# Moving the transposing DMA of K between the loads of K and Q and the load of V in a windowed-attention and maxout-FFN kernel

## The chip, the cores and the metric

One core of one Trainium2 chip. The metric is the device time of one execution in microseconds (us); the time before is the median of three runs. The core has the engines TensorE (PE; PEld is its weight load), VectorE (DVE), ScalarE (ACT), GpSimd (POOL) and SyncE (SP), and 16 DMA engines that take the transfers which SyncE and GpSimd issue.

## What is computed

Attention over 4 batches, 8 heads, 768 positions and a head size of 64. Each position sees the 128 positions up to its own (a sliding window) and the first 4 positions of the sequence (the sinks). The result, 3072 tokens of 512 values, goes through a feed-forward layer with three weight matrices of 512 x 768 and one of 768 x 512, the hidden value being the maximum of three products:

```python
scores = scale * np.matmul(q, k.transpose(0, 1, 3, 2))
keep = is_sink | in_window
a = softmax(np.where(keep, scores, -1e9))
x = heads_joined(np.matmul(a, v))            # 3072 x 512
h = np.maximum(np.maximum(x @ w1, x @ w2), x @ w3)
out = h @ w_out
```

## The kernel before

The 3072 tokens are cut into 12 chunks of 256, three to a batch. For each chunk the kernel loads K, Q and V (512 KB each, f32), casts them to bf16, transposes K and Q so that the head size lies on the partitions, computes scores, exponentials, masks and the weighted sum of V, transposes that sum (x_sb to xT), and runs the two layers of the feed-forward part.

The order of all instructions is written out by hand; each engine takes its own in the order of the program, and waits are put in only where data or a buffer calls for them. Up to chunk 3 the order is a long prologue. After that the loop `for i in range(3, NCH)` (L836) gives a slot to each i, and a slot works on several chunks at once: the feed-forward hidden layer of chunk i, the attention of chunk n = i + 1, the output layer of chunk m = i - 1, the cast and transpose of chunk i + 2, and the loads of chunk i + 3. Slots 4 to 10 take the branch that begins behind the `else`; the change is in that branch. A slot is named by its i below.

These parts matter for the change:

- `load(ci, what)` (L93, its DMA at L107) issues on SyncE's queue one transfer of 512 KB for each letter of `what`, by default K, then Q, then V. It does nothing for a chunk from 12 on. The raw f32 tiles have two buffers for each of K, Q and V (the pool `raw`, L51), so a load needs the cast of the chunk two before it to be over.
- `cast(ci)` (L605) is POOL's work: eight casts of K (`cast_k`, L85, at L90), then V in eight casts (`cast_v`, L121, at L129; for the chunks that the later slots cast). Where the chunk is the second of its batch, a small copy of the first keys into `ks` (`sink_k`, L278, at L283) stands between the two, and that one reads the transposed K of the chunk before. Q is cast by ACT from chunk 7 on (L953, `cast_qk`, at L118).
- `turn_dma(ci, w)` (L177) issues on SyncE's queue a transposing DMA out of the bf16 tile into `kT` or `qT` (at L188 for the chunks concerned). For K it needs POOL's eight casts. `kT` and `qT` are rings of four (L71).
- `score(n, ...)` (L314, and `score4`, L339, with its matmuls at L357) reads `kT` of chunk n and of the chunk before, and `qT`. It is the first work of TensorE in a slot, behind two small matmuls for the sinks where there are any. So `kT` of chunk i + 2, issued in slot i, is first read at the start of slot i + 1.
- `xpose_dma(n)` (L496, at L498) transposes x_sb into xT on SyncE's queue near the end of the slot; `ffn_h` (L504, matmuls at L517) reads it some us into the next slot. `store(m)` (L588) writes the output of chunk m from the same queue.

SyncE's order in a slot of 4 to 8 is therefore: qT of chunk i + 2, the loads of K, Q and V of chunk i + 3, kT of chunk i + 2, xT of chunk i + 1, the store of chunk i - 1. In the program's text the load stands at L936 and the transpose of K at L945, with `ffn_h` and `av` (other engines) between them.

Of the kernel before, what the change touches and what calls it, by code (L numbers as in the profile page):

```python
# [16 lines left out]
def kernel(  # L17
# [31 lines left out]
    with tc.manual_schedule():  # L49
# [30 lines left out]
        def keys(ci):  # L80

            return (kT[ci % RING].rearrange("q n p i r -> q (n p i r)")
                    .rearrange("q (p n h c) -> q p n h c", p=NP, n=2, h=2))
# [9 lines left out]
        def load(ci, what="kqv", gate=None, part=None, parts=1):  # L93
            if ci >= NCH:
                return
            b, c = divmod(ci, CPB)
            t0 = c * 256
            for w in what:
                src = {"k": k, "q": q, "v": v}[w]
                if (ci, w) not in raws:  # L100
                    raws[ci, w] = raw.tile([128, H, 2, D], F32, tag=w + "_raw", name=w + "_raw")
                dst = raws[ci, w]
                if gate is not None:
                    gate(dst[0:1, 0, 0, 0:1])
                n = H // parts
                for g in range(parts) if part is None else (part,):
                    nc.sync.dma_start(  # L107
                        out=dst[:, n * g:n * g + n],
                        in_=src[b, n * g:n * g + n, t0:t0 + 256]
                            .rearrange("h (p i) d -> p h (i d)", i=2))  # L110
# [66 lines left out]
        def turn_dma(ci, w):  # L177
            if ci >= NCH:
                return
            if w == "k" and ci < NEW:  # L180
                for n in range(2):
                    nc.sync.dma_start_transpose(
                        out=kT[ci % RING][:, n].rearrange("q p i r -> q (p i) r"),
                        in_=bfs[ci, w][64 * n:64 * n + 64].rearrange("q p i a d -> q (p i a d)"))
                return
            dst = (qT[ci % RING].rearrange("q p i n r -> q (p i) (n r)") if w == "q" else
                   keys(ci).rearrange("q p n h c -> q (p n) (h c)"))
            nc.sync.dma_start_transpose(  # L188
                out=dst, in_=bfs[ci, w].rearrange("s p i a d -> s (p i a d)"))
# [88 lines left out]
        def sink_k(b):  # L278
            x = (keys(b * CPB)[:, :, 0, 0].rearrange("q p (i r) -> q p i r", i=2) if b * CPB >= NEW else
                 kT[b * CPB][:, 0])  # L280
            for a in range(2):
                hp = slice(64 * a, 64 * a + 64)
                nc.gpsimd.tensor_copy(  # L283
                    ks[b % 2][hp, :, 4 * a:4 * a + 4].rearrange("q p (r i) -> q p r i", i=2),
                    x[hp, :, :, 0:2].rearrange("q p i r -> q p r i"))
# [106 lines left out]
        def expo(ci, p):  # L392
            if ci >= NEW:
                return expo4(ci, p)
            lo = 0 if ci % CPB else 1
            e, st = es[ci, p]
            for a in range(2):
                nc.scalar.activation(e[:, a, lo:], st[a][:, lo:], AF.Exp, scale=scale)  # L398
                give(st[a])
# [31 lines left out]
        def sink_v(b):  # L431

            x = vb[(b * CPB) % RING]
            sv = bank([128, 2, D + 1], F32, "sv")
            for a in range(2):
                for p in range(NP):
                    nc.tensor.matmul(
                        sv[32 * p:32 * p + 32, a], lhsT=(sel2 if b * CPB >= NEW else sel)[:, a], rhs=x[:, 0, 2 * p + a],
                        start=True, stop=True, tile_position=(0, 32 * p))
            nc.vector.tensor_copy(vs[b % 2], sv)  # L440
            give(sv)
# [129 lines left out]
        def fence():  # L571
            free.insert(0, home.pop(id(fences.pop()))[1])
# [263 lines left out]
        for i in range(3, NCH):  # L836
            n, m = i + 1, i - 1
            more = n < NCH
            if i == 3 or i >= NCH - 1:
                if more and n % CPB == 1:  # L840
                    if n < NEW:
                        sink_k(n // CPB)
                    sink_v(n // CPB)
                load(i + 3)
                cast(i + 2)
                turn_dma(i + 2, 'k')
                turn_dma(i + 2, 'q')
                if more:
                    sink_score(n)
                if more:  # L850
                    score(n, (0, 1))
                if more:
                    expo(n, 0)
                if more:
                    expo(n, 1)
                two = more and i > 3
                if two:
                    y_open(m)
                    y_turn(m, 0, 64 if n >= NEW else 128)
                else:  # L860
                    ffn_y(m, 0, nc.vector)
                if i == 3:
                    xpose(3, 0, nc.scalar)
                    xpose(3, 1, nc.scalar)
                if more:
                    score(n, (2,))
                if two:
                    fence()
                if more:
                    score(n, (3,))  # L870
                if more:
                    mask(n, 0)
                if more:
                    mask(n, 1)
                if more:
                    expo(n, 2)
                if two:
                    y_turn(m, 1, 64 if n >= NEW else 128)
                    y_out(m, 0, nc.vector)
                    y_out(m, 1, nc.vector)  # L880
                else:
                    ffn_y(m, 1, nc.vector)
                store(m)
                if more:
                    mask(n, 2)
                if more:
                    expo(n, 3)
                ffn_h(i, 0, 0)
                if more:
                    mask(n, 3)  # L890
                ffn_h(i, 0, 1)
                if more:
                    av_open(n); av(n, 0)
                ffn_h(i, 0, 2)
                if more:
                    av(n, 1)
                ffn_h(i, 1, 0)
                if more:
                    av(n, 2)
                ffn_h(i, 1, 1)  # L900
                if more:
                    av(n, 3); xpose_dma(n)
                ffn_h(i, 1, 2)
                ffn_h(i, 2, 0)
                ffn_h(i, 2, 1)
                ffn_h(i, 2, 2, 1 if i + 2 < NCH else 2)
            else:
                if more and n % CPB == 1:
                    if n < NEW:
                        sink_k(n // CPB)  # L910
                    sink_v(n // CPB)
                if more:
                    sink_score(n)
                cast(i + 2)
                turn_dma(i + 2, 'q')
                score(n, (0,))
                expo(n, 0)
                score(n, (3,))
                y_open(m)
                y_turn(m, 0, 64 if n >= NEW else 128)  # L920
                expo(n, 3)
                score(n, (1,))
                expo(n, 1)
                mask(n, 0)
                fence()
                score(n, (2,))
                y_turn(m, 1, 64 if n >= NEW else 128)
                mask(n, 3)
                expo(n, 2)
                mask(n, 1)  # L930
                y_out(m, 0, nc.vector)
                y_out(m, 1, nc.scalar)
                av_open(n)
                av(n, 0)
                mask(n, 2)
                load(i + 3)  # L936
                ffn_h(i, 1, 0)
                ffn_h(i, 0, 0)
                if more:
                    av(n, 1)  # L940
                ffn_h(i, 1, 2)
                ffn_h(i, 0, 1)
                if more:
                    av(n, 2)
                turn_dma(i + 2, 'k')  # L945
                if more:
                    av(n, 3)
                ffn_h(i, 1, 1)
                ffn_h(i, 2, 0)
                ffn_h(i, 0, 2)  # L950
                if NEW < i + 3 < NCH:
                    for g in range(2):
                        cast_qk(i + 3, "q", g, nc.scalar)  # L953
                ffn_h(i, 2, 1)
                if more:
                    xpose_dma(n)
                ffn_h(i, 2, 2, 1 if i + 2 < NCH else 2)
                store(m)
# [43 lines left out]
```

## Time and profile before

| what | value |
|---|---|
| median of three runs | 177.16 us (176.55 to 177.21) |
| the profiled execution | 177.08 us |
| its span, first to last instruction | 175.4 us |
| TensorE busy | 167.2 us, 95% |
| TensorE's granted clock | 0.999 |
| DMA moved | 34.95 MB, mean 199 GB/s |
| SyncE's DMA queue (q1) | 64784 packets, 31.33 MB |

The predictions' views are these. The page gives the busy time of each engine and the costliest groups. The view of waits names, for each engine and line, who ended its idle time, with the total in us, the number of times and the longest. The timeline lists instructions in order: start, time taken, engine, line, operation, output and inputs, and in square brackets the idle time of the engine before it and what ended that. A row with SPq is a DMA issue of SyncE; its second number is how long the issue took, not how long the transfer took. The view of DMA issues gives for each kind the count, the size and the time from the start of the issue to the landing of the data. Landing minus issue is thus time in the queue and on the way together.

### The profile page before, as it was taken

Reading aid. Unit: us, or ns where it says so; the run is one execution under the profiler, and the core shown is the slowest. Engines: PE = TensorE matmul, PEld = TensorE weight load, DVE = VectorE, ACT = ScalarE, POOL = GpSimd, SP = SyncE. Lnnn points to the kernel's source line nnn. Section 1 sums busy time; section 2 is a strip of 40 time slices with the busy share of each in tenths; the row PEclk is TensorE's granted clock in tenths of the full one; section 3 lists DMA queues with packets and bytes.
Section 4 is the critical chain, followed back from the end, with each engine's and each line's share of the span. In section 5 each row is a group of like instructions: output and inputs, shape, how many; then the busy total and the mean of one; then the engine's idle time right before and its main releaser. Section 6 shows DMA issues by size and latency. Waiting matters only on the chain.

```text
span 175.4 us, 5437 instructions
## 1 busy us (share of the span) xinstructions
PE 167.2 (95%) x2228; PEld 129.3 (74%) x2233; DVE 124.3 (71%) x262; ACT 89.6 (51%) x185; POOL 110.0 (63%) x193
## 2 busy tenths in 40 slices
PE   7979999999999999999999999997999999999992
PEld 2446879857696696797797797795797797796871
DVE  3387854896697894886877977875977777776452
ACT  4778544677945814817726627624726616510210
POOL 7399507546489999999999999586999700000000
PEclk9999999999999999999999999999999999999999
DMA  5999999999999999988999999899999605019303
GB/s 145 299 285 197 220 215 261 220 313 270 303 191 297 308 193 230 251 197 220 268 174 243 277 153 252 237 170 216 259 178 281 35 17 166 4 25 158 121 0 120
DMA packets 70505, 34.95 MB, mean 199 GB/s; under 512 B 26448, under 2 KB 68944, under 8 KB 70480
## 3 DMA queue, kind: packets, MB, share of 16 engines
q1 hardware_dynamic: 64784, 31.33, 80.4%
q0 software_dynamic: 5552, 3.15, 12.6%
q8 instruction: 17, 0.28, 0.7%
q10 hardware_dynamic: 144, 0.13, 0.2%
q14 instruction: 8, 0.07, 0.2%
HBM read 25.17 MB, written 6.29 MB: 179 GB/s over the span
## 4 chain that ended last, share of the span: by engine, by line
PE 59%; DMA 23%; POOL 9%; SPq 2%; issue 2%; ACT 2%; DVE 0%; POOLq 0%
PE h_ps L517 37%; PE y_ps L561 9%; DMA k_raw<-in_k_dram 5%; DMA kT<-k_bf 5%; DMA q_raw<-in_q_dram 4%; PE y_ps L537 4%; DMA w<-in_moe_w_dram 4%; PE o L471 3%; DMA v_raw<-in_v_dram 3%; PE st L357 3%; POOL vb L123 3%; DMA qT<-q_bf 3%; POOL vb L129 2%; POOL w L292 2%; SPq L107 1%
## 5 line engine op out<-in xcount | busy, mean ns | idle before, releaser
L517 PE MATMUL h_ps<-xT,w 128*128 128x256 bf16 x864 | 101.2, 273 | 0.5 <-DMA w<-in_moe_w_dram 0.4
L517 PEld LDWEIGHTS <-w 128*128 128x128 bf16 x864 | 81.9, 98 | 10.8 <-DMA w<-in_moe_w_dram 0.7
L527 DVE TENSOR_TENSOR h_sb<-h_sb,h_ps 128x512 bf16<-128x512 bf16 (+1 forms) x74 | 49.0, 669 | 17.8 <-PE h_ps L517 16.2
L523 ACT CAST h_sb<-h_ps 128x512 bf16<-128x512 f32 x35 | 20.6, 588 | 50.9 <-PE h_ps L517 50.8
L129 POOL CAST vb<-v_raw 32x512 bf16<-32x512 f32 x48 | 37.0, 771 | 2.3
L90 POOL CAST k_bf<-k_raw 32x512 bf16<-32x512 f32 x48 | 29.1, 607 | 4.3 <-issue 2.2
L398 ACT ACTIVATE e_sb<-st 128x512 bf16<-128x512 f32 (+1 forms) x48 | 23.2, 591 | 1.1 <-PE st L331 1.1
L479 DVE TENSOR_TENSOR x_sb<-o,rc 128x256 bf16<-128x256 f32 x48 | 20.4, 424 | 1.6
L561 PE MATMUL y_ps<-wo,h_sb 64*64 64x512 bf16 (+1 forms) x312 | 21.1, 377 | 0.0
L471 PE MATMUL o<-vb,e_sb 128*128 128x65 bf16 x352 | 16.5, 193 | 0.8 <-DVE vb L123 0.8
L471 PEld LDWEIGHTS <-e_sb 128*128 128x128 bf16 x352 | 14.5, 97 | 3.1 <-ACT e_sb L398 0.9
L123 POOL CAST vb<-v_raw 64x512 bf16<-64x512 f32 x18 | 13.1, 727 | 5.0 <-DMA v_raw<-in_v_dram 4.5
L406 DVE TENSOR_TENSOR e_sb<-e_sb,msk 128x1024 bf16<-128x1024 bf16 (+1 forms) x18 | 13.0, 747 | 3.4 <-ACT e_sb L398 3.4
L389 DVE TENSOR_TENSOR e_sb<-e_part,msk 128x1024 bf16<-128x1024 bf16 x16 | 12.9, 822 | 3.3 <-ACT e_part L374 3.1
L561 PEld LDWEIGHTS <-h_sb 64*64 64x64 bf16 (+1 forms) x312 | 9.9, 106 | 5.0
L374 ACT ACTIVATE e_part<-st 128x384 bf16<-128x384 f32 x32 | 13.1, 496 | 0.5 <-PE st L357 0.5
L537 PE MATMUL y_ps<-wo,h_sb 128*128 128x512 bf16 x49 | 12.6, 380 | 0.3
L476 DVE RECIPROCAL rc<-o 128x4 f32<-128x4 f32 x48 | 8.3, 174 | 4.0 <-PE o L471 4.0
L118 POOL CAST k_bf<-k_raw 128x512 bf16<-128x512 f32 x6 | 3.8, 648 | 9.1 <-PE h_ps L517 6.8
L118 ACT CAST q_bf<-q_raw 128x512 bf16<-128x512 f32 x13 | 7.6, 620 | 2.8 <-DMA q_raw<-in_q_dram 2.8
L537 PEld LDWEIGHTS <-h_sb 128*128 128x128 bf16 x54 | 4.9, 98 | 5.4 <-DVE h_sb L527 0.5
L427 ACT ACTIVATE e_sink<-sk 128x256 bf16<-128x256 f32 x8 | 3.1, 389 | 10.4 <-PE sk L423 10.4
(90 smaller groups left out, 144.3 us busy)
## 6 DMA issues: line engine op xcount, KB each, us to landing
k_raw<-in_k_dram SPq DMA_DIRECT2D x11, 512.0 KB, 5.6
v_raw<-in_v_dram SPq DMA_DIRECT2D x11, 512.0 KB, 7.8
out_dram<-y_sb SPq DMA_DIRECT2D x11, 512.0 KB, 3.2
q_raw<-in_q_dram SPq DMA_DIRECT2D x10, 512.0 KB, 7.5
w<-in_moe_w_dram POOLq DMA_DIRECT2D x9, 256.0 KB, 6.4
q_raw<-in_q_dram SPq DMA_DIRECT2D x4, 256.0 KB, 7.6
wo<-in_moe_w_out_dram POOLq DMA_DIRECT2D x2, 384.0 KB, 8.2
v_raw<-in_v_dram SPq DMA_DIRECT2D x2, 256.0 KB, 5.2
```

The source lines that it names most:

```text
L90: f(bfs[ci, "k"][x:x + 32, :, n], raws[ci, "k"][y:y + 32, :, i].rearrange("q (p a) d -> q p a d", a=2))
L123: eng.tensor_copy(vb[ci % RING][64 * i:64 * i + 64, n, :, 0:D], raws[ci, "v"][64 * n:64 * n + 64, :, i])
L129: eng.tensor_copy(vb[ci % RING][x:x + 32, n, :, 0:D], raws[ci, "v"][y:y + 32, :, i])
L374: nc.scalar.activation(dst, st[a], AF.Exp, scale=scale)
L398: nc.scalar.activation(e[:, a, lo:], st[a][:, lo:], AF.Exp, scale=scale)
L471: nc.tensor.matmul(o[:, t, a], lhsT=e[:, a, s], rhs=vb[cv % RING][:, n, 2 * p + a], start=first, stop=True, skip_group_check=True)
L479: nc.vector.tensor_mul(xs[ci][:, p], o[:, :, :, 0:D], rc.unsqueeze(3).to_broadcast([128, 2, 2, D]))
L517: nc.tensor.matmul(hp[:, f].rearrange("q (i t r) -> q i t r", i=2, r=x.shape[3]), lhsT=w_sb[wi][:, ds, c0:c0 + 128], rhs=x, start=(ds == 0 ...
L523: (nc.scalar.copy if eng is nc.scalar else eng.tensor_copy)(dst, hp)
L527: nc.vector.tensor_max(dst[:, x], dst[:, x], hp[:, x])
L537: nc.tensor.matmul(yp, lhsT=hs[ci][:, fb, t * 128:(t + 1) * 128], rhs=wo[:, fb], start=(fb == 0), stop=(fb == FB - 1))
L561: nc.tensor.matmul(yps[ci][t][c:c + cols], lhsT=hs[ci][hp, fb, x:x + cols], rhs=wo[hp, fb], start=(turn == 0 and fb == 0), stop=(turn == 1 ...
```

## The change

In slots 4 to 10 the call that issues the transposing DMA of K moves ahead of the load of V. The load is split in two calls for it. Nothing else is changed.

```diff
                 av_open(n)
                 av(n, 0)
                 mask(n, 2)
-                load(i + 3)
+                load(i + 3, 'kq')
+                turn_dma(i + 2, 'k')
+                load(i + 3, 'v')
                 ffn_h(i, 1, 0)
                 ffn_h(i, 0, 0)
                 if more:
@@
                 ffn_h(i, 0, 1)
                 if more:
                     av(n, 2)
-                turn_dma(i + 2, 'k')
                 if more:
                     av(n, 3)
```

SyncE's order in these slots becomes: qT of chunk i + 2, the loads of K and Q of chunk i + 3, kT of chunk i + 2, the load of V of chunk i + 3, xT of chunk i + 1, the store of chunk i - 1. For slot 9 there is no chunk 12 to load, and for slot 10 there is neither a load nor a chunk 12 to transpose.

## The prediction

> **What bounds the kernel now.** I read the page's busy times first, then TensorE's waits from 60 us on (when the twelve-chunk loop is in its steady part), then TensorE's own timeline around the one wait that is left.
>
> ```profile
> PE 167.2 (95%) x2228; PEld 129.3 (74%) x2233; DVE 124.3 (71%) x262; ACT 89.6 (51%) x185; POOL 110.0 (63%) x193
> ```
>
> ```profile
> PE st L357 <- DMA kT<-k_bf: 0.9, 1, 0.9
> PE sk L423 <- DMA qT<-q_bf: 0.2, 1, 0.2
> ```
>
> TensorE is busy 95% of the span. The second fence is the whole answer on its waits after 60 us: two waits, 0.9 us for a transposed K and 0.2 us for a transposed Q. An edit that only moves a DMA can win no more there than what TensorE waits for, so the first fact is a ceiling of about 1 us out of 177. The next fence is TensorE's timeline around the larger wait.
>
> ```profile
> 115.18 4.53 PE L517 MATMUL h_ps<-xT,w 128*128 128x256 bf16 x40
> 120.64 0.52 PE L357 MATMUL st<-qT,kT 64*64 64x256 bf16 x16 [0.93 <-DMA kT<-k_bf]
> ...
> 124.34 1.91 PE L517 MATMUL h_ps<-xT,w 128*128 128x256 bf16 x16
> ...
> 133.13 0.53 PE L357 MATMUL st<-qT,kT 64*64 64x192 bf16 x24
> ```
>
> The forty matmuls of chunk 7's slot end at 115.18 + 4.53 = 119.71. The scores of chunk 9, the first work of slot 8, start at 120.64: 0.93 us of nothing. Slot 9's scores start at 133.13. Why K of chunk 9 was late stands in SyncE's own timeline (start, time that the issue took) and in the landing column of the DMA issues of the same stretch.
>
> ```profile
> 108.24 0.64 SPq L107 DMA_DIRECT2D q_raw<-in_q_dram  x1
> 108.98 3.46 SPq L107 DMA_DIRECT2D v_raw<-in_v_dram  x1
> 112.53 3.26 SPq L188 DMA_TRANSPOSE kT<-k_bf  x1
> 116.81 1.55 SPq L498 DMA_TRANSPOSE xT<-x_sb  x1
> ...
> 119.75 1.88 SPq L188 DMA_TRANSPOSE qT<-q_bf  x1
> 121.69 0.74 SPq L107 DMA_DIRECT2D k_raw<-in_k_dram  x1
> 122.47 0.63 SPq L107 DMA_DIRECT2D q_raw<-in_q_dram  x1
> 123.21 1.16 SPq L107 DMA_DIRECT2D v_raw<-in_v_dram  x1
> 124.48 3.48 SPq L188 DMA_TRANSPOSE kT<-k_bf  x1
> ```
>
> Landings after the issue, first of slot 7 (issues of 107 to 115 us), then of slot 8 (121 to 127 us), then the one xT of 116.81:
>
> ```profile
> q_raw<-in_q_dram SPq DMA_DIRECT2D x1, 512.0 KB, 7.7
> v_raw<-in_v_dram SPq DMA_DIRECT2D x1, 512.0 KB, 9.2
> ...
> kT<-k_bf SPq DMA_TRANSPOSE x1, 8.1
> ```
>
> ```profile
> k_raw<-in_k_dram SPq DMA_DIRECT2D x1, 512.0 KB, 4.8
> q_raw<-in_q_dram SPq DMA_DIRECT2D x1, 512.0 KB, 5.8
> v_raw<-in_v_dram SPq DMA_DIRECT2D x1, 512.0 KB, 8.3
> qT<-q_bf SPq DMA_TRANSPOSE x1, 4.3
> kT<-k_bf SPq DMA_TRANSPOSE x1, 7.9
> ```
>
> ```profile
> xT<-x_sb SPq DMA_TRANSPOSE x1, 4.6
> ```
>
> Adding issue and landing: in slot 7 Q lands at 115.9, V at 118.2, kT at 120.6, xT at 121.4. In slot 8 K lands at 126.5, Q at 128.3, V at 131.5, kT at 132.4. Transfers of SyncE's queue land in the order of issue, so kT pays for all of V ahead of it.
>
> **The change part by part.** Nothing is computed differently and no instruction is added or removed. In slots 4 to 8 two issues on SyncE trade places, the load of V (chunk i+3) and the transpose of K (chunk i+2). In slot 9 no load is left (there is no chunk 12), and in slot 10 neither exists, so nothing moves there.
>
> **kT gets earlier.** Without V ahead, kT follows Q. Behind V it needed 132.4 - 131.5 = 0.9 us in slot 8 and 120.6 - 118.2 = 2.4 us in slot 7. Taking these as the two ends of its own time, the new landing in slot 7 is between 115.9 + 0.9 = 116.8 and 115.9 + 2.4 = 118.3, both ahead of the 119.71 at which TensorE is ready. I take the later end, since it is this slot's own. The 0.93 us then goes whole. The ends of the gain are 0 (if kT keeps all of the 120.6 - 115.9 = 4.7 us that it now needs after Q) and 0.93 (nothing else waits there); a loss is priced under the rivals.
>
> **What is late next at 119.71.** The rest of SyncE's work, and POOL, ACT and DVE, have to let TensorE run 0.93 us earlier from there on.
>
> ```profile
> 105.75 6.37 POOL L129 CAST vb<-v_raw 32x512 bf16<-32x512 f32 x8
> 114.33 5.17 POOL L90 CAST k_bf<-k_raw 32x512 bf16<-32x512 f32 x8 [2.21 <-issue]
> 120.71 0.44 POOL L283 COPY ks<-kT 64x16 bf16<-64x16 bf16 x2 [1.21 <-DMA kT<-k_bf]
> 121.22 6.17 POOL L129 CAST vb<-v_raw 32x512 bf16<-32x512 f32 x8
> ```
>
> ```profile
> 117.61 1.14 ACT L118 CAST q_bf<-q_raw 128x512 bf16<-128x512 f32 x2
> 121.04 2.12 ACT L374 ACTIVATE e_sb<-st 128x384 bf16<-128x384 f32 x5 [2.29 <-PE st L357]
> ```
>
> ACT sits idle 2.29 us before the exponentials, waiting for the scores, so they follow. xT (chunk 8) landed at 121.4 and is first read at 124.34; 0.93 us earlier that is 123.41, still 2.0 us behind the landing. Slot 8's kT landed at 132.4 against a need of 133.13, which becomes 132.20: in the old order 0.2 us of the gain would be given back there. In the new order it lands at 128.3 + 0.9 to 128.3 + 2.4, that is 129.2 to 130.7, and does not matter. From 133 us on the loads are over and no wait of TensorE stands in the list.
>
> **V gets later.** It is now behind kT, by kT's 0.9 to 2.4 us. In slot 7 V would land between 119.1 and 120.6. Its reader is POOL's cast, which now starts at 121.22; that start is itself 1.21 us late, because POOL stands in front of it waiting for the same kT (the copy into ks). Without that wait the cast could start at 114.33 + 5.17 + 0.44, about 120.0. So POOL waits at most 0.6 us for V where it waited 1.21 us for kT: no loss, and the cast's result is needed only two slots after the load. Cost taken: 0; if the cover goes, POOL falls behind by what V is late beyond 1.2 us.
>
> **The wait that stands in SyncE's order.** kT carries a wait for POOL's eight casts of K, and V, xT, the store and the next qT are queued behind it. In slot 7 these casts were over before 105.75, when POOL began on V; SyncE reaches the place behind Q at 108.24 + 0.64, about 108.9. In slot 8 they end at 114.33 + 5.17 = 119.50, and SyncE gets there at 123.1. So SyncE would find the K ready by 3.2 and 3.6 us, and the wait costs 0. The Trainium skill, "DMA: Bandwidth & Descriptors", section "Anatomy of one DMA — SWDGE (gpsimd) path", speaks against the move: a DMA's wait is served on the issuing sequencer before dispatch, so a transfer that waits holds back those issued after it, needed or not. By that rule V would pay for a late POOL; these rows show a POOL that is not late, so the sum stays, and the rule's other outcome is the third rival below.
>
> **xT.** The pair V and kT took SyncE from 108.98 to 115.79, and xT went out at 116.81. It can go when the DVE has written x_sb:
>
> ```profile
> 116.32 0.42 DVE L479 TENSOR_TENSOR x_sb<-o,rc 128x256 bf16<-128x256 f32 x1
> ```
>
> That is 116.74, so SyncE was not what held it, by 0.9 us. The bytes ahead of xT are the same in either order. Cost 0; without the cover each us would count only beyond the 2.0 us above.
>
> **Sum.** The profiled execution took 177.08 us (span 175.4, and 1.7 around it). Less 0.93 that is 176.15. It stood 0.08 under the median of the runs, 177.16, so the forecast on the runs' scale is **176.2**. The three runs lie 0.66 us apart (176.55 to 177.21), so a wait of this size may not be in each of them; I take 175.8 to 176.7 as the forecast's own range. About 0.5% (0.9 us) is what a measurement of this kernel can tell from no change, and the whole gain is about that.
>
> **Rival 1: kT is late for another reason than V (0.22).** A view of the DMA from 115 to 121 us shows how little was moved while kT was under way (40 slices of 0.15 us, GB/s):
>
> ```profile
> GB/s 345 311 333 251 217 179 135 72 27 20 20 20 24 15 19 72 130 9 10 10 137 394 247 239 234 118 12 0 5 9 7 12 9 10 183 90 278 295 543 301
> ...
> q14 instruction: 1, 0.01, 2.1%
> q8 instruction: 1, 0.02, 1.0%
> ```
>
> For most of 116 to 120 the engines moved 0 to 30 GB/s with two instruction fetches among their work. If a fetch on one of the 16 engines holds up a transpose that runs over all of them, kT may stay in flight until 120.6 wherever it stands in the queue. For it: 2.4 us behind V here against 0.9 in slot 8. Against it: with V out of the way kT is through Q at 115.9 and has 3.8 us until 119.71, more than the 2.4. Time: no gain, **177.1**, 176.7 to 177.5.
>
> **Rival 2: five transposes in the middle of the loads make the DMA queue the bound (0.15).** A load behind a transpose is slower to land than one behind a load: in slot 8 K landed 126.5 - 124.05 = 2.4 us after qT, Q only 1.8 us after K. That is 0.6 us more, and the new order puts V behind kT in five slots: 5 x 0.6 = 3.0 us of queue. If all of it reached TensorE (through xT, or through next loads), the time would be 177.1 - 0.9 + 3.0 = **179.2**. It decides from the point at which the queue has less than 0.6 us of idle time a slot. Against it speaks how xT lands from 60 to 140 us:
>
> ```profile
> L498 SPq DMA_TRANSPOSE xT<-x_sb x6: 1232/1232/2200, 65.8 to 130.1; - x6
> ...
> DMA to landing us min/median/max: 3.1/3.1/4.6
> ```
>
> The median is the minimum: most xT find the queue empty, and only one or two stand behind something. Two slots of 0.6 us are 1.2, inside the 2.0 us that xT has.
>
> **Rival 3: SyncE is held at kT (0.05).** If POOL ran over 3.6 us later than in the rows, SyncE would stand at kT with V, xT, the store and the next qT behind it. xT has 2.0 us more, so the first us is lost when POOL is 6.6 us late: 176.2 + 1.0 = **177.2**, and more beyond.
>
> **How the numbers follow.** Forecast 0.58, rivals 0.22, 0.15, 0.05. The forecast lies on the edge of 0.5% (176.27): of its 0.58 I give 0.42 to faster and 0.16 to the same. Rival 1 gives 0.20 to the same and 0.02 to slower, rival 2 0.15 to slower, rival 3 0.02 and 0.03. That makes faster 0.42, same 0.38, slower 0.20. The range 175.8 to 177.6 holds the forecast and rival 1 and leaves out rival 2 and the far end of rival 3.
>
> **What would show it.** Right: the profile after has no wait of PE for kT; kT in slots 4 to 8 lands 1 to 3 us after Q and ahead of V; POOL's 1.21 us wait for kT is gone or has become a shorter one for V; the span is 174.5. Wrong: a wait of PE st for kT still near 120 us with kT in flight over 4 us behind Q (rival 1); xT landing over 3.1 us after its issue in most slots and waits of h_ps for xT (rival 2); SyncE standing in front of kT for POOL (rival 3).

## The result and the profile after

| | before | after |
|---|---|---|
| median of 22 runs each | 176.62 us (175.88 to 178.22) | 176.13 us (175.80 to 177.03) |
| profiled execution | 177.08 us | 176.05 us |
| span | 175.4 us | 174.3 us |

The ratio after to before is 0.9963, with a 95% interval of 0.9946 to 0.9981: faster by 0.37%, which is 0.65 us. The two medians differ by 0.49 us, and the interval, 0.34 to 0.95 us, holds both. The forecast was 0.93 us and 176.2. The prediction called a change of less than 0.5% the same: by that border the measured 0.37% counts as the same, although its interval leaves out no change at all. In the profiled execution 1.0 us went.

The change shows first in SyncE's timeline of slot 7, after: kT stands between Q and V.

```profile
108.17 0.71 SPq L107 DMA_DIRECT2D q_raw<-in_q_dram  x1
108.98 4.96 SPq L188 DMA_TRANSPOSE kT<-k_bf  x1
113.98 0.58 SPq L107 DMA_DIRECT2D v_raw<-in_v_dram  x1
116.76 1.23 SPq L498 DMA_TRANSPOSE xT<-x_sb  x1
```

Their landings, counted from the issue, after (DMA issues of 107.5 to 114.5 us, then the one xT):

```profile
q_raw<-in_q_dram SPq DMA_DIRECT2D x1, 512.0 KB, 7.6
v_raw<-in_v_dram SPq DMA_DIRECT2D x1, 512.0 KB, 5.8
kT<-k_bf SPq DMA_TRANSPOSE x1, 7.6
```

```profile
xT<-x_sb SPq DMA_TRANSPOSE x1, 3.9
```

Q lands at 108.17 + 7.6 = 115.8, kT at 116.6, V at 119.8, xT at 120.7. Before, kT landed at 120.6. It is 4.0 us earlier in these two executions, of which only the first 0.9 us can be used. TensorE's timeline, after, across the same place:

```profile
115.12 4.53 PE L517 MATMUL h_ps<-xT,w 128*128 128x256 bf16 x40
119.58 0.52 PE L357 MATMUL st<-qT,kT 64*64 64x256 bf16 x16
```

No bracket, so no idle time: the scores of chunk 9 follow the matmuls of slot 7 directly. The view of TensorE's waits from 69 us on is empty in this profile. POOL's timeline, after, shows where V's delay went:

```profile
100.47 5.16 POOL L90 CAST k_bf<-k_raw 32x512 bf16<-32x512 f32 x8
106.91 6.90 POOL L129 CAST vb<-v_raw 32x512 bf16<-32x512 f32 x8 [1.27 <-DMA v_raw<-in_v_dram]
114.16 5.17 POOL L90 CAST k_bf<-k_raw 32x512 bf16<-32x512 f32 x8 [0.35 <-POOL vb L129]
119.40 0.45 POOL L283 COPY ks<-kT 64x16 bf16<-64x16 bf16 x2
119.90 0.61 POOL L129 CAST vb<-v_raw 32x512 bf16<-32x512 f32 x1
```

POOL's 1.21 us in front of the ks copy are gone. Instead it now stands 1.27 us ahead of 106.91, for the V that slot 6 loaded. Before, it idled 2.21 us ahead of 114.33; the profile names no releaser there, but the next K landed at 107.40 + 6.8 = 114.2. So the new wait is taken out of that one, of which 0.35 us is left, and the K casts start at 114.16, no later than they did.

### The profile page after: what moved, and what is told of

It reads as the page before. It is cut to its first block, busy times and chain, and to the rows that moved or that the text cites. A ratio compares the mean times of both kernels' runs of the same rounds, so it can differ in the third digit from the quotient of the medians.

```text
span 174.3 us, 5433 instructions
## 1 busy us (share of the span) xinstructions
PE 167.1 (96%) x2228; PEld 129.3 (74%) x2233; DVE 124.6 (71%) x262; ACT 89.6 (51%) x185; POOL 110.5 (63%) x193
## 4 chain that ended last, share of the span: by engine, by line
PE 68%; DMA 18%; POOL 7%; issue 2%; SPq 1%; ACT 1%; DVE 0%; POOLq 0%
PE h_ps L517 43%; PE y_ps L561 11%; DMA k_raw<-in_k_dram 4%; DMA q_raw<-in_q_dram 4%; PE o L471 4%; DMA w<-in_moe_w_dram 4%; PE y_ps L537 4%; PE st L357 3%; DMA v_raw<-in_v_dram 3%; DMA qT<-q_bf 3%; POOL vb L123 3%; POOL w L292 2%; SPq L107 1%; PE st L331 1%; POOL k_bf L118 1%
## 5 line engine op out<-in xcount | busy, mean ns | idle before, releaser
L517 PE MATMUL h_ps<-xT,w 128*128 128x256 bf16 x864 | 101.2, 273 | 0.6 <-DMA w<-in_moe_w_dram 0.4
L517 PEld LDWEIGHTS <-w 128*128 128x128 bf16 x864 | 81.8, 98 | 11.0 <-DMA w<-in_moe_w_dram 0.9
L129 POOL CAST vb<-v_raw 32x512 bf16<-32x512 f32 x48 | 37.5, 781 | 4.0 <-DMA v_raw<-in_v_dram 1.3
L389 DVE TENSOR_TENSOR e_sb<-e_part,msk 128x1024 bf16<-128x1024 bf16 x16 | 13.4, 862 | 3.1 <-ACT e_part L374 3.0
```

Source lines behind the costliest of these rows:

```text
L129: eng.tensor_copy(vb[ci % RING][x:x + 32, n, :, 0:D], raws[ci, "v"][y:y + 32, :, i])
L389: nc.vector.tensor_mul(x.rearrange("q a (t s) c -> q (a t) s c", t=2), y, msk2)
L517: nc.tensor.matmul(hp[:, f].rearrange("q (i t r) -> q i t r", i=2, r=x.shape[3]), lhsT=w_sb[wi][:, ds, c0:c0 + 128], rhs=x, start=(ds == 0 ...
```

## Experiments

The question was whether the one wait of TensorE is the whole difference, why only 0.65 us of 0.93 came, and whether place or bytes decide. All ratios are against the kernel before in the same set of runs. A second measure turned out to be far sharper than the clock: **the stretch** from TensorE's first sink scores of slot 4 to the end of its last matmul. Two rows of TensorE's timeline give it, here for the kernel after:

```profile
68.28 0.29 PE L423 MATMUL sk<-qT,ks 128*32 128x256 bf16 x4
...
169.52 1.47 PE L583 MATMUL y_ps<-wo,h_sb 128*128 128x256 bf16 x12
```

169.52 + 1.47 - 68.28 = 102.71 us; from unrounded times 102.72. It leaves out the prologue, whose end, read as the start of the stretch, moved between 68.1 and 71.0 us from one profiled execution to the next, more than the effect sought.

**kT ahead of V in slot 7 alone** (shown against the kernel before).

```diff
-                load(i + 3)
+                early = i == 7
+                load(i + 3, 'kq')
+                if early:
+                    turn_dma(i + 2, 'k')
+                load(i + 3, 'v')
...
-                turn_dma(i + 2, 'k')
+                if not early:
+                    turn_dma(i + 2, 'k')
```

> kT ahead of V in slot 7 alone, the old order in slots 4, 5, 6 and 8. Theory (the one wait behind slot 7 is the whole difference): as fast as the change, ratio about 0.996 to 0.998 against before, no wait of TensorE for kT of chunk 9; slot 8, in the old order, may give back up to 0.2 us. Rival (the gain comes from the sum of small shifts of transfers in all five slots): ratio within 0.999 to 1.001.

Measured: 0.9990 (0.9966 to 1.0013), which doesn't tell the theories apart. The stretch does: 102.72 us, that of the full change. kT in slot 7 landed 109.76 + 6.8 = 116.6 against 109.03 + 6.6 = 115.6 for Q:

```profile
109.03 0.63 SPq L107 DMA_DIRECT2D q_raw<-in_q_dram  x1
109.76 4.04 SPq L188 DMA_TRANSPOSE kT<-k_bf  x1
```

```profile
q_raw<-in_q_dram SPq DMA_DIRECT2D x1, 512.0 KB, 6.6
...
kT<-k_bf SPq DMA_TRANSPOSE x1, 6.8
```

No wait for kT anywhere, and slot 8, in the old order, gave nothing back. Moving one transfer in one slot does all that the change does in five.

**kT ahead of V in slots 4, 5, 6 and 8, not in 7.** The same edit with the other condition:

```diff
+                early = i != 7
```

> The change in slots 4, 5, 6 and 8, the old order in slot 7. Theory: no gain, ratio 0.999 to 1.001, and a wait of TensorE for kT near 120 us as in the kernel before wherever V is slow there. Rival (sum of small shifts): most of the gain, ratio about 0.997.

Measured: 1.0023 (0.9995 to 1.0051); the stretch is 103.23 us. TensorE's timeline has the wait again (this execution, with 179.28 us the longest of its twelve runs, reached slot 4 only at 71.0 us, so its times lie later):

```profile
122.82 0.53 PE L357 MATMUL st<-qT,kT 64*64 64x256 bf16 x16 [0.44 <-DMA kT<-k_bf]
```

102.72 plus 0.44 is 103.16, so the wait explains the stretch but for 0.07 us. The shifts in the other four slots bring nothing that shows.

**kT ahead of Q as well** (against the kernel after).

```diff
-                load(i + 3, 'kq')
+                load(i + 3, 'k')
                 turn_dma(i + 2, 'k')
-                load(i + 3, 'v')
+                load(i + 3, 'qv')
```

> kT goes one load further ahead, between K and Q. Theory: kT lands another 1.8 us earlier, which TensorE has no use for, so the time is that of the change (ratio against before about 0.996); SyncE reaches kT 0.7 us sooner and still finds K cast, except in slot 4, where the casts end within 0.1 us or so of it. Rival (SyncE is held at kT by POOL and all behind it is late): slower than the change by 0.3 us or more, with V and Q landing later and POOL or ACT waiting for them.

Measured: 0.9997 (0.9974 to 1.0020); the stretch is 102.71 us, and TensorE waits for nothing after 60 us. A still earlier kT has no further use, as the theory said. By the clock the theory missed: about 0.996 lies below the interval, and a loss of 0.3 us against the change, the rival's, lies in it. But the rival's mechanism isn't in the trace: with no wait of TensorE and the stretch of the change, nothing that the edit touches cost time in the profiled execution. Its prologue, the same code, ended late (slot 4 at 70.2 us). That the clock's shortfall is the prologue's in the other runs too is likely and not shown.

**V in halves, one ahead of kT and one behind** (against the kernel after).

```diff
                 load(i + 3, 'kq')
+                load(i + 3, 'v', part=0, parts=2)
                 turn_dma(i + 2, 'k')
-                load(i + 3, 'v')
+                load(i + 3, 'v', part=1, parts=2)
```

> V is loaded in two halves of 256 KB, the first ahead of kT, the second behind it; same bytes, one issue more in a slot. Theory (what is ahead of kT in the queue sets its landing): kT lands between the two kernels, in slot 7 about 0.9 us later than in the change, near 117.5, still ahead of the 119.6 at which TensorE is ready, so no wait and the stretch from slot 4 to TensorE's end as long as in the change (102.7 us). Rival (a transpose inside the loads of a slot is what helps, wherever; or the wait is an accident): no such order of landings.

Measured: 0.9973 (0.9941 to 1.0005), stretch 102.71 us, no wait. kT's issue and landing in slot 7:

```profile
112.48 2.64 SPq L188 DMA_TRANSPOSE kT<-k_bf  x1
```

```profile
kT<-k_bf SPq DMA_TRANSPOSE x1, 6.2
```

It landed at 112.48 + 6.2 = 118.7; this execution was 1.1 us later at slot 4 than the one of after, so that is 117.6 on its scale: between 116.6 and 120.6, and 1.0 us behind that of the change where 0.9 was expected. On the same scale the second profile of after, below, has its kT at 115.8, 0.8 us earlier than the first, so the safer reading is kT's landing behind Q's in the same execution: 0.8 to 0.9 us with kT ahead of V (three profiles), 2.5 with half of V ahead (118.7 less 116.2), 3.3 to 4.7 with all of V ahead (seven profiles).

**One more load of 512 KB, ahead of kT or behind it.** V is loaded a second time into a tile that nobody reads (the function `extra`, which issues this load, is left out below). First in the order of before, against the kernel before:

```diff
                 load(i + 3)
+                extra(i + 3)
```

> The order of before, and one more load of 512 KB (V again, into a tile that nobody reads) between V and kT in slots 4 to 8. Theory: kT lands about 1.8 us later in each of these slots, and where the margin is below that TensorE waits for it: in slots 4 to 8 the margins were 1.6, 1.5, 2.0, -0.9 and 0.8 us, so waits for kT of 0.2, 0.3, 0, up to 2.7 and 1.0 us, each shortened by the waits before it; 2 to 4 us more than before, ratio 1.012 to 1.023. Rival (the bytes in the queue are what counts, not the place): as slow as the same load behind kT.

Then in the changed order, against the kernel after:

```diff
                 load(i + 3, 'v')
+                extra(i + 3)
```

> The changed order, and the same additional load of 512 KB behind V, so behind kT, in slots 4 to 8. Theory (place counts): kT lands as early as in the change, no wait of TensorE for kT; what is pushed is xT, the store and the next qT and K, by up to 1.8 us a slot, which xT's 2 us cover in part: time within 1 us of the change, at least 1.5 us faster than the load ahead. Rival (bytes count, the DMA queue is full): as slow as with the load ahead, through late K and kT of the next slots.

Measured: 1.0246 (1.0178 to 1.0314) ahead, 1.0135 (1.0025 to 1.0244) behind. TensorE's waits from 60 us on, ahead:

```profile
PE st L357 <- DMA kT<-k_bf: 3.9, 4, 1.4
PE sk L423 <- DMA qT<-q_bf: 0.4, 1, 0.4
```

and behind (the new function stands nine lines long above, so L517 is L526 here):

```profile
PE h_ps L526 <- DMA xT<-x_sb: 2.6, 1, 2.6
PE st L357 <- DMA kT<-k_bf: 1.3, 2, 0.7
PE h_ps L526 <- ACT y_sb L584: 0.4, 1, 0.4
```

Ahead, the theory's sum holds, with waits for kT of 3.9 us against 2 to 4, but not its parts: behind slots 4 to 8 TensorE waited 0, 1.45, 0.27, 1.22 and 0.95 us, where 0.2, 0.3, 0, up to 2.7 and 1.0 were expected. Behind, most of my expectation failed. The waits for kT shrink to 1.3 us, as place demands, but are not gone; xT is late by 2.6 us, and in the two profiled executions the stretches are alike (106.68 and 107.21 us). By the clock the load behind stands at about 1% less than the load ahead, with intervals that overlap: its four runs took 178.17, 178.37, 180.74 (the profiled one) and 181.08 us. So the 2.6 us may not be in each execution. They came once, in front of slot 9's first matmuls with xT, while an instruction fetch was long as well:

```profile
133.07 2.94 SPq L507 DMA_TRANSPOSE xT<-x_sb  x1
140.81 1.92 PE L526 MATMUL h_ps<-xT,w 128*128 128x256 bf16 x16 [2.57 <-DMA xT<-x_sb]
```

```profile
q14 instruction: 1, 0.01, 2.8%
```

(The last row is of the DMA view of 137 to 141 us, where 2.8% of 16 x 4 us is 1.8 us.) How xT lands, with the load behind:

```profile
L507 SPq DMA_TRANSPOSE xT<-x_sb x6: 1777/2874/4093, 66.0 to 133.1; - x6
...
DMA to landing us min/median/max: 4.4/5.9/7.7
```

and in the kernel after without it:

```profile
L498 SPq DMA_TRANSPOSE xT<-x_sb x6: 1232/1233/2008, 65.9 to 129.1; - x6
...
DMA to landing us min/median/max: 3.0/3.6/4.4
```

In the order of the slots these landings are 4.9, 4.4, 5.7, 6.1, 6.7 and 7.7 us: from the second on they grow. So both count: place decides which reader waits, and in either of the two places another 512 KB a slot is more than the queue can take without a wait of TensorE.

**POOL's ks copy behind V's casts**, in the order of before.

```diff
-            if ci > NEW and ci % CPB == 1:
-                sink_k(ci // CPB)
             for n in range(2):
                 for i in range(2):
                     cast_v(ci, n, i, nc.gpsimd)
+            if ci > NEW and ci % CPB == 1:
+                sink_k(ci // CPB)
```

> The order of before; POOL makes the copy into ks behind V's casts and not ahead of them, so that it no longer stands 1.2 us waiting for kT of chunk 9 ahead of V's casts. Theory (the gain is TensorE's own wait): time as before, ratio 0.998 to 1.002, the wait of TensorE near 120 us still there. Rival (the gain came through POOL, whose later casts were released earlier): as fast as the change.

Measured: 1.0029 (0.9992 to 1.0065), so no gain by the clock. But the profiled execution had no wait of TensorE either, with a stretch of 102.72 us, which the theory had not said. That opened the question whether the old order always has the wait. It was profiled again, with the kernel before three times more and the kernel after once more:

> The kernel before, unchanged, for a second profile of it. Theory (kT of chunk 9 lands late because V is ahead of it, by an amount that varies between executions): TensorE again has a wait of st for kT between 119 and 121 us, of 0 to 1 us, kT in slot 7 again 4 us or more behind Q, or else the wait is smaller by as much as kT follows V faster (0.9 instead of 2.4 us). Rival (the wait is an accident of the one profile and no part of the time): no wait at all, and the same time as in the first profile, 177.1.

> The kernel before, unchanged, a third profile. Two had TensorE waiting 0.93 and 0.74 us for kT of chunk 9, with 103.7 and 103.5 us from slot 4 to TensorE's end; the order of before with the ks copy late had no wait, 102.7 us, its kT landing 0.4 us ahead of need. Theory (the old order puts kT's landing within about 1 us of the need, on either side, by how instruction fetches fall on the DMA engines): a wait between 0 and 1 us, and the stretch 102.7 us plus the wait. Rival (the wait is fixed in the old order, and moving the ks copy took it away): 0.7 to 0.95 us again.

> The kernel before, unchanged, a fourth profile; expected as for the third. Over the four, theory: not all waits alike, and at least one well below 0.7 us or none. Rival: all between 0.7 and 0.95 us.

> The order of before with POOL's ks copy behind V's casts, a second profile. Theory (its missing wait was one side of a margin of a few tenths): kT of chunk 9 lands within 1 us of the need again, a wait of 0 to 0.9 us. Rival (the ks copy was a cause of the wait): again no wait, kT 0.4 us or more ahead.

> The changed kernel once more. Theory: kT of chunk 9 lands 0.85 to 0.95 us behind Q and 2 us or more ahead of the need, no wait of TensorE after slot 4 begins, 102.7 us from there to its end. Rival: a wait of some tenths here as well.

All twelve executions without the additional load, with the wait for kT in front of slot 8's scores, and the share that one instruction fetch (queue q14, 8 KB) has of the 16 DMA engines between 114.5 and 122.5 us (1% of 16 x 8 us is 1.3 us):

| slot 7 in | kernel | wait, us | stretch, us | q14 |
|---|---|---|---|---|
| the old order | before | 0.93 | 103.72 | 1.6% |
| | before, second | 0.74 | 103.53 | 1.4% |
| | before, third | 0 | 102.71 | 0.2% |
| | before, fourth | 0.92 | 103.70 | 1.7% |
| | ks copy late | 0 | 102.72 | 0.2% |
| | ks copy late, second | 1.02 | 103.81 | 1.5% |
| | all but slot 7 | 0.44 | 103.23 | 0.2% |
| the new order | after | 0 | 102.72 | 0.2% |
| | after, second | 0 | 102.72 | 0.3% |
| | slot 7 alone | 0 | 102.72 | 0.2% |
| | kT ahead of Q | 0 | 102.71 | 0.3% |
| | V in halves | 0 | 102.71 | 0.2% |

The rows that carry it, the scores of chunk 9 in TensorE's timeline and q14 in the DMA view, for the third and the fourth profile of before:

```profile
120.80 0.52 PE L357 MATMUL st<-qT,kT 64*64 64x256 bf16 x16
```

```profile
q14 instruction: 1, 0.01, 0.2%
```

```profile
120.36 0.52 PE L357 MATMUL st<-qT,kT 64*64 64x256 bf16 x16 [0.92 <-DMA kT<-k_bf]
```

```profile
q14 instruction: 1, 0.01, 1.7%
```

For the second profile of before the profile names another releaser, but kT's landing fits, at 112.25 + 8.1 = 120.35:

```profile
112.25 3.34 SPq L188 DMA_TRANSPOSE kT<-k_bf  x1
```

```profile
kT<-k_bf SPq DMA_TRANSPOSE x1, 8.1
```

```profile
120.45 0.53 PE L357 MATMUL st<-qT,kT 64*64 64x256 bf16 x16 [0.74 <-DVE h_sb L527]
```

In every row the stretch is 102.7 us plus the wait, to 0.1 us. The wait comes and goes in the old order and did not come in the new one. The ks copy is no cause: the same kernel had 0 and 1.02. For the kernel before the four waits average (0.93 + 0.74 + 0 + 0.92) / 4 = 0.65 us, and 0.37% of 176.62 is 0.65 us. That the two agree to the hundredth is chance: four profiles are few, the interval reaches from 0.34 to 0.95 us, and the three kernels with the stretch of the change came out at 0.9990, 0.9997 and 0.9973 by the clock.

Where the fetch of q14 took 1.4% to 1.7% (about 2 us) the wait was 0.7 to 1.0 us; where it took 0.2% the old order had 0, 0 and 0.44. In the packets of the trace the long ones begin 0.4 to 0.7 us before Q of slot 7 has landed, with V still to come, and V then lands 2.2 us behind Q; the short ones begin when V has landed, 1.6 to 1.7 us behind Q. Whether the fetch holds up V, or V the fetch, no run here settles: no kernel changed the fetch by itself.

Another fetch, of 16 KB on queue q8, tells more. In the ten profiles with all of Q or V ahead of kT there are 50 landings of kT in slots 4 to 8. Where no q8 fetch was in flight in the first 0.8 us behind the landing of the transfer ahead (32 of them), kT landed 0.8 to 1.0 us behind that transfer. Where one was (18), it landed 1.6 to 2.5 us behind it, but for one of 0.9. Before, the fetch falls into kT's turn in slots 4 and 7; after, into that of slot 6 alone, where kT landed at 96.06 + 9.3 = 105.4 against 95.24 + 7.7 = 102.9 for Q. The DMA view of before from 118 to 121 us, behind the landing of V in slot 7, and that of after from 102.9 to 105.3 us, behind the landing of Q in slot 6:

```profile
q8 instruction: 1, 0.02, 2.1%
```

```profile
q8 instruction: 1, 0.02, 2.7%
```

After, from 115.8 to 116.6 us, in kT's turn of slot 7, the view has no q8. So in slot 7 the change took kT out from behind V, and also out of the way of this fetch.

## Why the prediction was right, and where its sizes were off

- **The number.** 176.2 against 176.13 is closer than the parts deserve, and that is luck. The forecast started from 177.16, the median of three runs; over 22 runs it is 176.62. The start was 0.54 us too high and the gain 0.28 us too large by the ratio, 0.44 by the medians. From 176.62 the same sum would have given 175.7, just below the forecast's own range.
- **The bound and the ceiling.** Right. TensorE's waits after 60 us were the whole of what the change could win. The stretch went from 103.72 to 102.72 us, and the one wait was 0.93.
- **kT gets earlier.** Right, and more so than taken. I gave kT 2.4 us behind Q, as slot 7 showed behind V; it took 0.8 (116.6 less 115.8), and 0.8 to 0.9 in slots 4, 5 and 8 as well. The 2.4 us were not the transfer's own time, and not slot 7's own either: they went with the q8 fetch, and came again in slot 6 in the new order, where kT had time to spare.
- **The wait goes whole.** Right for an execution that has it. As the size of the change it was too large: the profile had one of the longer waits, and a fourth of the profiles of before had none. I had the hint, runs 0.66 us apart, and used it for the range and not for the forecast. 0.65 us was measured, not 0.93; the interval alone does not exclude 0.93, but the old order without a wait in one profile of four does exclude 0.93 in each execution.
- **What is late next.** Nothing was: from the start of slot 4's stretch on TensorE waits for nothing in both profiles of after. The 0.2 us that slot 8 was to give back in the old order did not show, in the run with slot 7 alone.
- **V gets later.** The cost of 0 was right, the reason too narrow. I looked at slot 7; the delay came out in slot 6, as 1.27 us of POOL, and POOL's idle time before the next K casts took it in. Another wait of 0.56 us stands ahead of POOL's casts at 131.86, where V of slot 8 had landed at 131.8; TensorE did not wait for it.
- **SyncE's wait in front of kT.** Right: in slot 7 Q's issue ends at 108.88 and kT's begins at 108.98, and in slots 4 to 8 alike there are 0.1 us between the two. So the third rival did not come up. The Trainium skill, "DMA: Bandwidth & Descriptors", section "Anatomy of one DMA — SWDGE (gpsimd) path", says that a DMA's wait is served on the issuing sequencer. In these slots there was none to serve, so this case does not test it.
- **The first rival** (kT late for a reason other than V) is out as it stood, since kT moved 4.0 us with its place. It had a true core: kT's landing is late by about 1.5 us where a fetch of q8 falls into its turn, and in slot 7 the old order put it there in all seven profiles. Whether TensorE then waited went with how early Q and V had landed, and mostly with how long the fetch of q14 took: 0.7 to 1.0 us in the four profiles with a long one, 0, 0 and 0.44 in the three with a short one.
- **The second rival** (the queue as the bound) did not decide, and its 3.0 us of queue did not show. The later of kT and V landed behind Q by 4.0, 2.5, 2.9, 4.7 and 4.1 us in slots 4 to 8 before, 18.2 in all, and by 4.0, 2.7, 3.9, 4.0 and 2.7 after, 17.3 in all. One of its signs came: four of six xT took more than 3.1 us to land (median 3.6, before 3.1), without a wait of TensorE. The room that I had given xT, 2.0 us, was about right: with the additional load xT landed 7.7 us after its issue at 133.07, 4.6 more than 3.1, and 2.57 of these became a wait.

## What to carry to other kernels

A transfer that the critical engine waits for belongs ahead of bulk loads that nobody needs for a slot, and the gain ends where the wait ends: kT came 4 us earlier for at most 0.9 us of time. Before a wait of under 1 us is taken as the size of a gain, look at several profiles of the kernel before, because a landing close to its need falls on either side of it. And where the start of a program varies by more than the effect, compare a stretch between two fixed instructions and not the whole time.

## What the runs showed of the hardware

The issue of a transposing transfer is not a fixed cost to SyncE: kT took 4.96 us in slot 7, after, and xT 1.23 us in the same slot, while the load of V between them took 0.58 us. With one more load ahead of it the median issue of xT went from 1.23 to 2.87 us, as the rows on xT above show, so the time moved with what stood in the queue and is no price of the instruction alone. One 8 KB instruction fetch, on the same DMA engines as the data, took 0.2% of 128 us, some 0.3 us, in the third profile of before, and 1.7%, some 2.2 us, in the fourth. And a transposing transfer that landed 0.8 to 1.0 us behind the transfer ahead of it landed 1.6 to 2.5 us behind it in 17 of the 18 cases in which a 16 KB fetch was in flight in its turn. That the fetch is the cause is likely, since moving kT changed which slot had the delay; no run moved the fetch by itself.
